# A mixing product's sums of two terms, made by accumulating DMA in place of VectorE

## The chip, the cores and the metric

The kernel runs on one core of a Trainium2 chip. The metric is the device time of one execution in microseconds (us). Engines are called PE (TensorE, matmuls), DVE (VectorE), ACT (ScalarE), POOL (GpSimd) and SP (SyncE, which here only issues DMA). SP and POOL each feed a DMA queue of their own; both queues use the same 16 DMA engines.

## The reference

Three layers, each on the output of the one before, all in float32:

```python
# 1: x (4, 3072, 256): FFT along the sequence, complex mixing, soft threshold, inverse
X = rfft(x, axis=1)
Yr = Xr @ w_r - Xi @ w_i + b_r;  Yi = Xr @ w_i + Xi @ w_r + b_i
Y = sign(Y) * max(abs(Y) - 0.01, 0)          # for each part
x = irfft(Yr + 1j * Yi)
# 2: gated layer with a product along the sequence
h = max(x @ w_in, 0);  u, v = h[..., :512], h[..., 512:]
v_n = (v - mean(v)) / sqrt(var(v) + 1e-6)
v_s = einsum('ts,bsd->btd', w_spatial, v_n) + b_spatial[None, :, None]
x = (u * v_s) @ w_out
# 3: on tokens
g = s * max(x @ w_in2, 0) ** 2 + b
out = g @ w_out2
```

The change lies at the product of `w_spatial` (3072 x 3072) with `v_n` (3072 x 512 for each of four batches), called the mixing product.

## The kernel before

Three stages follow each other: `attention` (the FFT layer, u's input, and v normalized and stored as `vn`), `mixing` (the mixing product), and `output` (everything behind it). The order of instructions on each engine is that of the program; no scheduler moves any.

Mixing computes a 2x2-block product by seven products in place of eight, twice nested. A round is one of the seven outer products; its left factor is a block of `w_spatial` or a sum or difference of several, its right factor the same of `vn` blocks. `OUTER` (line 707) lists, for each round in order (1, 5, 2, 6, 3, 7, 4), the first term of each factor, the second term with its operator, and the name under which the sum is kept for a later round (s1, s2, t1, t2). Inside a round, seven inner products (`INNER`, in the order 2, 5, 3, 1, 6, 7, 4) of six steps each run on the round's quarters. So a round has 42 steps, counted 0 to 41 here, and the stage 294. A step (`multiply`, line 847) is 24 matmuls.

A quarter is six tiles: a11 to a22 are the left factor's (128x768, 384 KB a tile), b11 to b22 the right factor's (128x512, 256 KB). There is one set of them. As soon as a quarter's last use in a round is over (`LAST`), its tiles are loaded again for the next round; `FIRST_USE` gives the inner product in which it is needed there. a12 comes free from step 10 on, a11 from 16, b21 and b12 from 22, a21 and b11 from 28, a22 and b22 from 34, one tile of each a step.

What step n issues, in this order: the 24 matmuls; ACT's rounded high parts of step n + 2 (`high`); DVE's inner sums of step n + 3 (`sums`); at the end of an inner product, `evacuate` for two of four accumulators; DVE's low parts of step n + 2 (`low`); `evacuate` for the other two; the sums of two outer terms (`outer_sums`); a weight conversion, if one is under way; the loads that are due (`loads`).

`evacuate` (line 865) either copies an accumulator into a `kept` tile on ACT (line 877), or adds it to one on DVE (line 873) and stores that to `md` through POOL (line 874). The kept tiles are few: those that ACT writes after a round's first inner product (step 5) are read by the product stores after its fourth (step 23), are written again at step 35, and are read again by the product stores of step 41. So the next round's step 5 can write them once these have landed.

A tile with two terms takes two loads through SP, into the quarter and into a staging tile `st_a` or `st_b` (three of each, lines 765 and 771). Three steps later DVE adds them (line 774), and if the sum is kept, POOL stores it (line 776). `loads` counts the sums under way and leaves further loads of that kind for later steps. Terms by round:
- rounds 1 (outer product 5) and 3 (outer product 6): two terms for all 48 tiles, all sums kept
- round 4 (product 3): two for a only; round 5 (product 7): two for a and b; round 6 (product 4): two for b only; no sum kept
- rounds 0 and 2: one term

The loads of a round run during the round before it.

Of the kernel before, what the change touches and what calls it, by code (L numbers as in the profile page):

```python
# [227 lines left out]
def attention(tc, nc, x, w_r, w_i, b_r, b_i, c_f, c_b, c_g, c_v, c_s, zd, vd, yd, vn, chunks, cd, follow, nb=NB):  # L228
# [338 lines left out]
    def v_product():  # L567

        n = v_done[0]
        v_done[0] += 1  # L570
        y = y_hl[n // 3]
        o = (n % 3) * 128
        pool, tag = (pm, "pm") if tail[0] and n % 2 else (pa, "pa")
        ps = pool.tile([128, 512], F32, tag=tag, name="ps_vp")
        c = 0
        for k in range(2):
            for a, w in PASSES:
                nc.tensor.matmul(ps, y[:, a, k, o:o + 128], win[k][:, w, :], start=c == 0, stop=c == 5)  # L578
                c += 1
        vr = vpool.tile([128, 512], F32, tag="vr", name="vr", bufs=VR)  # L580
        bn = vpool.tile([128, 6], F32, tag="bn", name="bn")
        j = n % 3
        if j == 0:
            grp[0] = (vpool.tile([128, 3, 2], F32, tag="mv", name="mv"),
                      vpool.tile([128, 5, 3], F32, tag="rs", name="rs"), [])
        mv, t, vrs = grp[0]
        vrs.append(vr)
        va, r, z, root, nmr = (t[:, m, :] for m in range(5))

        def stats():  # L590
            nc.vector.bn_stats(bn, vr)  # L591
            nc.vector.bn_aggr(mv[:, j, :], bn)

        def spread():
            nc.vector.tensor_scalar_add(va, mv[:, :, 1], EPS)

        def rstd():
            nc.vector.reciprocal(r, root)
            for _ in range(2):
                nc.vector.tensor_mul(z, r, r)  # L600
                nc.vector.scalar_tensor_tensor(out=z, in0=z, scalar=-0.5, in1=va, op0=ALU.mult, op1=ALU.mult)
                nc.vector.scalar_tensor_tensor(out=r, in0=z, scalar=1.5, in1=r, op0=ALU.add, op1=ALU.mult)
            nc.vector.scalar_tensor_tensor(out=nmr, in0=mv[:, :, 0], scalar=-1.0, in1=r, op0=ALU.mult, op1=ALU.mult)

        def normal(m):
            if m == 0 or m == 2 and n // 3 % 2 == 0:
                nc.scalar.activation(vrs[m], vrs[m], AF.Identity, bias=nmr[:, m:m + 1], scale=r[:, m:m + 1])
            else:
                nc.vector.tensor_scalar(vrs[m], vrs[m], r[:, m:m + 1], nmr[:, m:m + 1], op0=ALU.mult, op1=ALU.add)

        def store():
            b, i = divmod(n - 2, 24)
            for m in range(3):
                nc.gpsimd.dma_start(out=vn[b][i + m], in_=vrs[m])
        ch.step()
        nc.scalar.activation(vr, ps, AF.Relu)
        rest = [wait, stats]
        if j == 2:
            rest += [spread, lambda: nc.scalar.sqrt(root, va), rstd, lambda: (normal(0), normal(1)),
                     lambda: normal(2), store]  # L620
        ch.add(rest)
# [82 lines left out]

OUTER = {
# [7 lines left out]
}  # L715
INNER = (2, 5, 3, 1, 6, 7, 4)

# [12 lines left out]
def mixing(tc, nc, ws, vn, md, sd, convert_half):  # L730
# [31 lines left out]
    def load(g, name, i):  # L762
        first, then = OUTER[outer[g]][0 if name[0] == "a" else 2:][:2]
        t = q[name, i]
        nc.sync.dma_start(out=t, in_=source(first, name, i))
        if then is None:
            return
        op, second, kept = then
        n = t.shape[1]
        s = banks[2].tile([128, n], F32, tag="st_" + name[0], name="st_" + name[0], bufs=3)  # L770
        nc.sync.dma_start(out=s, in_=source(second, name, i))

        def add():
            nc.vector.tensor_tensor(out=t, in0=t, in1=s, op=getattr(ALU, op))
            if kept:
                nc.gpsimd.dma_start(out=sd[kept][int(name[1]) - 1, int(name[2]) - 1, i], in_=t)
        added.append((now[0], name[0], add))

    todo = []

    def loads():

        n = {"a": 3, "b": 3}
        for _, kind, _ in added:
            n[kind] -= 1
        for x in sorted(todo):
            g, _, i, name = x
            if OUTER[outer[g]][1 if name[0] == "a" else 3] is not None:
                if n[name[0]] <= 0:
                    continue  # L790
                n[name[0]] -= 1
            todo.remove(x)
            load(g, name, i)

    def outer_sums(age):
        while added and added[0][0] <= now[0] - age:
            added.pop(0)[2]()

    sub, add = nc.vector.tensor_sub, nc.vector.tensor_add
    term, hl = {}, {}  # L800
# [95 lines left out]
    def run():  # L896
# [12 lines left out]
        for n in range(total):  # L909
            now[0] = n  # L910
            multiply(n)
            ends = n % NS == NS - 1
            if n + 2 < total:
                high("a", n + 2)
                high("b", n + 2)
            if n + 3 < total:
                sums(n + 3)
            if ends:
                evacuate(n, 0)
                evacuate(n, 1)  # L920
            if n + 2 < total:
                low("a", n + 2)
                low("b", n + 2)
                freed(n + 2)
            if ends:
                evacuate(n, 2)
                evacuate(n, 3)
            outer_sums(3)
            if conversion and (todo or n % 3 == 2):
                conversion.pop()()  # L930
            loads()
            if n >= 6 and not conversion and not added and not todo and n % 3 == 0:
                conversion = [x for x in [convert_half(stage)] if x]
# [11 lines left out]
def output(tc, nc, yd, md, chunks, cd, bs, s_in, b_in, out):  # L945
# [43 lines left out]
    def combine(n):  # L989

        c = blocks[n][3]
        into = mixed[n] = m[{"11": 2, "12": 3, "22": 5, "21": 4}[c]]
        sums = {"11": ((2, 1, 2),), "12": ((6, 1, 6), (3, 3, 5), (3, 3, 6)),
                "22": ((7, 6, 7), (5, 5, 7)), "21": ((4, 4, 7),)}[c]
        t = bias_t[n].unsqueeze(1).to_broadcast([128, 2, TH])
        return [z for e in (0, 2) for z in [
            lambda e=e, o=o, x=x, y=y: nc.vector.tensor_add(o[:, e:e + 2], x[:, e:e + 2], y[:, e:e + 2])
            for o, x, y in ((m[o], m[x], m[y]) for o, x, y in sums)] + [
            lambda e=e: nc.vector.tensor_tensor(out=into[:, e:e + 2], in0=into[:, e:e + 2], in1=t, op=ALU.add)]]

    y_t, bias_t = {}, {}
# [223 lines left out]
```

## Time and profile before

| | |
|---|---|
| time, median of 3 runs | 3201.36 us (3199.89 to 3202.3) |
| profiled execution | 3198.43 us, span 3196.7 us |
| mean granted clock of PE | 0.987 of full speed |
| PE busy | 3085.7 us, 97% of the span |
| DVE busy | 2309.5 us, 72% |
| ACT busy | 1428.3 us, 45% |
| POOL busy | 392.8 us, 12% |
| HBM read, written | 322.72 MB, 162.53 MB |
| mixing stage (first to last matmul of line 856) | 559 to 1832 us |

Matmuls are pipelined, so "busy" on PE does not say how many it starts; the number of matmuls in a window does. A window's DMA share is the mean busy share of the 16 DMA engines, and can stand a little over 1. The granted clock is that of PE, as a share of its full speed.

### The profile page before, as it was taken

To read this page: it belongs to the slowest core of one execution; us is meant where nothing else is said; L and a number is where in the kernel's file an instruction comes from. 1 tells how busy PE (TensorE), PEld (TensorE's weight loads), DVE (VectorE), ACT (ScalarE), POOL (GpSimd) and SP (SyncE) were. 2 spreads that over 40 slices of the span, in tenths; PEclk is the share of its full clock that TensorE was granted. 3 is DMA by queue.
4 is the path that set the end of the run, shared out by engine and by line. 5 is a ranking of instruction groups with operands and counts; after the bars stand their busy time and mean duration, and the time that the engine had idled before them with its cause. 6 is when DMAs were issued, how large, how long until landed. Compare 5 with 4: busy or idle time off the path is not lost.

```text
span 3196.7 us, 46508 instructions
## 1 busy us (share of the span) xinstructions
PE 3085.7 (97%) x17960; PEld 3012.8 (94%) x17960; DVE 2309.5 (72%) x3495; ACT 1428.3 (45%) x2244; POOL 392.8 (12%) x497
## 2 busy tenths in 40 slices
PE   6989998999999999999999999999999999999999
PEld 5888986999999999999999989999999999999999
DVE  5877988787878888888878755656566656656564
ACT  5776766433434333434434334444444444444443
POOL 2665544021000210000000100000000000000000
PEclk7999999999999999999999999999999999999999
DMA  8987659487456956466471621111111111110210
GB/s 245 291 263 228 228 184 322 162 314 288 159 198 200 359 212 233 148 217 246 158 238 44 239 82 55 48 50 65 55 65 55 65 55 65 55 64 29 70 45 15
DMA packets 230517, 488.30 MB, mean 153 GB/s; under 512 B 22356, under 2 KB 116376, under 8 KB 230296
## 3 DMA queue, kind: packets, MB, share of 16 engines
q1 hardware_dynamic: 197224, 353.51, 33.4%
q0 software_dynamic: 33072, 131.82, 11.2%
q8 instruction: 140, 2.29, 0.3%
q14 instruction: 81, 0.66, 0.1%
HBM read 322.72 MB, written 162.53 MB: 152 GB/s over the span
## 4 chain that ended last, share of the span: by engine, by line
PE 76%; DVE 13%; DMA 5%; ACT 3%; issue 2%; POOL 0%; SPq 0%; ACTq 0%; DVEq 0%; POOLq 0%
PE acc L856 28%; PE ps_h L1066 17%; PE oacc L1087 17%; PE ps_o L1047 4%; PE ps_u L1029 4%; PE ps_m L413 3%; PE ps_vp L578 2%; DMA st_a<-in_moe_w_spatial_dram 2%; DVE a_hl L837 1%; DVE kept L873 1%; DMA st_b<-vn 1%; DVE b_hl L837 1%; DMA st_b<-t 1%; PE ps_g L366 1%; DVE bn L591 1%
## 5 line engine op out<-in xcount | busy, mean ns | idle before, releaser
L856 PE MATMUL acc<-a_hl,b_hl 128*128 128x384 f32 x7056 | 1239.5, 336 | 32.7 <-DVE kept L873 13.3
L856 PEld LDWEIGHTS acc<-a_hl,b_hl 128*128 128x128 f32 x7056 | 1232.9, 189 | 39.3 <-ACT kept L877 13.0
L1066 PE MATMUL ps_h<-x_hl,w 128*128 128x384 f32 x3072 | 580.8, 337 | 1.5 <-ACT x_hl L1050 0.9
L1087 PE MATMUL oacc<-q_hl,w 128*128 128x384 f32 x3072 | 575.4, 336 | 0.6 <-DVE q_hl L1073 0.6
L1066 PEld LDWEIGHTS ps_h<-x_hl,w 128*128 128x128 f32 x3072 | 543.3, 188 | 2.1 <-ACT x_hl L1050 1.3
L1087 PEld LDWEIGHTS oacc<-q_hl,w 128*128 128x128 f32 x3072 | 537.0, 188 | 0.9 <-DVE q_hl L1073 0.8
L833 ACT CAST a_hl<-a 128x768 fp32r<-128x768 f32 x253 | 211.7, 837 | 524.1 <-PE acc L856 436.7
L1073 DVE TENSOR_TENSOR q_hl<-r,q_hl 128x768 fp32r<-128x768 f32 x256 | 245.4, 959 | 230.7 <-ACT q_hl L1072 230.7
L1071 DVE TENSOR_TENSOR r<-r 128x768 f32<-128x768 f32 x256 | 244.8, 956 | 204.4 <-ACT r L1070 204.4
L1072 ACT CAST q_hl<-r 128x768 fp32r<-128x768 f32 x256 | 213.7, 835 | 301.8 <-DVE r L1071 301.8
L1070 ACT ACTIVATE r<-ps_h 128x768 f32<-128x768 f32 x256 | 208.3, 814 | 310.6 <-PE ps_h L1066 307.2
L837 DVE TENSOR_TENSOR a_hl<-a,a_hl 128x768 fp32r<-128x768 f32 x253 | 241.4, 954 | 137.5 <-ACT a_hl L833 137.0
L837 DVE TENSOR_TENSOR b_hl<-b,b_hl 128x512 fp32r<-128x512 f32 x295 | 202.0, 685 | 0.0
L833 ACT CAST b_hl<-b 128x512 fp32r<-128x512 f32 x295 | 181.8, 616 | 0.0
L578 PE MATMUL ps_vp<-win,y_hl 128*128 128x512 f32 x576 | 154.5, 404 | 18.3 <-ACT v_sb L444 15.0
L874 POOL DMA_DIRECT2D md<-kept x112 | 60.7, 542 | 828.4 <-DVE kept L873 824.0
L1029 PE MATMUL ps_u<-y_hl,w 128*128 128x384 f32 x768 | 145.7, 339 | 1.8 <-DVE y_hl L1015 1.8
L1047 PE MATMUL ps_o<-g,w 128*128 128x384 f32 x768 | 139.2, 337 | 1.6 <-DVE g L1037 1.0
L578 PEld LDWEIGHTS ps_vp<-win,y_hl 128*128 128x128 f32 x576 | 102.1, 190 | 40.4 <-ACT v_sb L444 16.8
L1029 PEld LDWEIGHTS ps_u<-y_hl,w 128*128 128x128 f32 x768 | 135.5, 190 | 3.1 <-DVE y_hl L1015 2.1
L1047 PEld LDWEIGHTS ps_o<-g,w 128*128 128x128 f32 x768 | 133.4, 188 | 2.6 <-DVE g L1037 1.6
L873 DVE TENSOR_TENSOR kept<-acc,kept 128x768 f32<-128x768 f32 x112 | 102.9, 952 | 22.1 <-PE acc L856 21.1
(139 smaller groups left out, 3700.7 us busy)
## 6 DMA issues: line engine op xcount, KB each, us to landing
a<-in_moe_w_spatial_dram SPq DMA_DIRECT2D x144, 384.0 KB, 5.0
b<-vn SPq DMA_DIRECT2D x168, 256.0 KB, 5.3
md<-kept POOLq DMA_DIRECT2D x112, 384.0 KB, 5.3
m<-md SPq DMA_DIRECT2D x56, 768.0 KB, 5.6
st_a<-in_moe_w_spatial_dram SPq DMA_DIRECT2D x72, 384.0 KB, 6.4
vn<-vr POOLq DMA_DIRECT2D x96, 256.0 KB, 4.0
s<-a POOLq DMA_DIRECT2D x48, 384.0 KB, 5.8
x_f<-in_x_dram SPq DMA_DIRECT2D x32, 384.0 KB, 6.5
```

What stands on the lines that cost most here:

```text
L578: nc.tensor.matmul(ps, y[:, a, k, o:o + 128], win[k][:, w, :], start=c == 0, stop=c == 5)
L833: nc.scalar.copy(s[:, 0, :], t)
L837: sub(s[:, 1, :], term.pop((kind, n)), f(s)[:, 0, :])
L856: nc.tensor.matmul(acc[d][:, h, 0:TH], b[:, m, d * 128:(d + 1) * 128], a[:, w, h * TH:(h + 1) * TH], start=fresh and i == 0 and c == 0, st ...
L1029: nc.tensor.matmul(ps[:, d, 0:TH], win[k][:, a, o:o + 128], y[:, w, k, :], start=c == 0, stop=c == 5)
L1047: nc.tensor.matmul(ps[:, h, 0:TH], wo[k // 2][:, a, o:o + 128], g[:, w, k, :], start=c == 0, stop=c == 11)
L1066: nc.tensor.matmul(ps[:, e, 0:TH], w[:, a, o:o + 128], x[:, i, j, :], start=c == 0, stop=c == 5)
L1070: nc.scalar.activation(r, ps[:, :, 0:TH], AF.Relu)
L1071: nc.vector.tensor_mul(r, r, r)
L1072: nc.scalar.copy(s[:, 0], r)
L1073: nc.vector.tensor_sub(s[:, 1], r, f(s)[:, 0])
L1087: nc.tensor.matmul(ps[:, h, 0:TH], w[:, a, o:o + 128], s[:, i, e, :], start=ff == 0 and c == 0, stop=ff == 2 * NP - 1 and c == 2)
```

## The change

A second term is no longer loaded into a staging tile and added by DVE. Its DMA adds to the quarter's tile directly (`accum_op=ALU.add`), issued by POOL four steps behind the first term's load. The store of a kept sum follows three steps behind that, also by POOL. `loads` no longer counts sums under way; it takes up to three loads a step. Since such a DMA only adds, the subtractions are made by signs: half of the `vn` blocks are stored negated (the second Newton step of the normalization multiplies two constants by the sign), and `combine` in the output stage takes the signs back (`tensor_sub` for `tensor_add` in places, as many instructions as before).

```diff
-            for _ in range(2):
+            for s in (1.0, sign):      # sign = -1.0 if (b < 2) == (i >= 12) else 1.0
                 nc.vector.tensor_mul(z, r, r)
-                nc.vector.scalar_tensor_tensor(out=z, in0=z, scalar=-0.5, in1=va, ...)
-                nc.vector.scalar_tensor_tensor(out=r, in0=z, scalar=1.5, in1=r, ...)
+                nc.vector.scalar_tensor_tensor(out=z, in0=z, scalar=-0.5 * s, in1=va, ...)
+                nc.vector.scalar_tensor_tensor(out=r, in0=z, scalar=1.5 * s, in1=r, ...)
...
-        op, second, kept = then
-        n = t.shape[1]
-        s = banks[2].tile([128, n], F32, tag="st_" + name[0], name="st_" + name[0], bufs=3)
-        nc.sync.dma_start(out=s, in_=source(second, name, i))
-
-        def add():
-            nc.vector.tensor_tensor(out=t, in0=t, in1=s, op=getattr(ALU, op))
-            if kept:
-                nc.gpsimd.dma_start(out=sd[kept][int(name[1]) - 1, int(name[2]) - 1, i], in_=t)
-        added.append((now[0], name[0], add))
+        second, kept = then
+
+        added.append((now[0] + 4, lambda: nc.gpsimd.dma_start(out=t, in_=source(second, name, i), accum_op=ALU.add)))
+        if kept:
+            added.append((now[0] + 7, lambda: nc.gpsimd.dma_start(
+                out=sd[kept][int(name[1]) - 1, int(name[2]) - 1, i], in_=t)))
...
-        n = {"a": 3, "b": 3}
-        for _, kind, _ in added:
-            n[kind] -= 1
-        for x in sorted(todo):
-            g, _, i, name = x
-            if OUTER[outer[g]][1 if name[0] == "a" else 3] is not None:
-                if n[name[0]] <= 0:
-                    continue
-                n[name[0]] -= 1
-            todo.remove(x)
+        for g, _, i, name in sorted(todo)[:3]:
+            todo.remove((g, FIRST_USE[name], i, name))
             load(g, name, i)
...
-    def outer_sums(age):
-        while added and added[0][0] <= now[0] - age:
-            added.pop(0)[2]()
+    def outer_sums():
+
+        for x in [x for x in added if x[0] <= now[0]]:
+            added.remove(x)
+            x[1]()
...
-        sums = {"11": ((2, 1, 2),), "12": ((6, 1, 6), (3, 3, 5), (3, 3, 6)),
-                "22": ((7, 6, 7), (5, 5, 7)), "21": ((4, 4, 7),)}[c]
+        sums = {"11": ((minus, 2, 1, 2),), "12": ((minus, 6, 6, 1), (plus, 3, 3, 5), (minus, 3, 3, 6)),
+                "22": ((minus, 7, 6, 7), (minus, 5, 7, 5)), "21": ((minus, 4, 7, 4),)}[c]
```

How this moves instructions is shown at three places of round 0. On SP, the loads of b21 and b12 from step 22 on, before (st_b is the staging tile, vn0 to vn3 the four batches' `vn`):

```order
L765 DMA b21_6353<-vn2_71 128x512
L771 DMA st_b_8421<-vn0_69 128x512
L765 DMA b12_6365<-vn3_72 128x512
L771 DMA st_b_8424<-vn1_70 128x512
L765 DMA b21_6354<-vn2_71 128x512
L771 DMA st_b_8470<-vn0_69 128x512
L765 DMA b21_6355<-vn2_71 128x512
L771 DMA st_b_8545<-vn0_69 128x512
```

and after:

```order
L770 DMA b21_6353<-vn2_71 128x512
L770 DMA b12_6365<-vn3_72 128x512
L770 DMA b21_6354<-vn2_71 128x512
L770 DMA b12_6366<-vn3_72 128x512
L770 DMA b21_6355<-vn2_71 128x512
L770 DMA b12_6367<-vn3_72 128x512
```

The staging loads are gone from SP, and b12's tiles come one a step instead of waiting for free staging.

On DVE, the accumulators' last evacuation of round 0 (step 41; line 873 before, 868 after) with what stands around it, before:

```order
L774 TENSOR_TENSOR a22_6338<-a22_6338,st_a_9043 128x768
L774 TENSOR_TENSOR b12_6369<-b12_6369,st_b_9046 128x512
L774 TENSOR_TENSOR b11_6376<-b11_6376,st_b_9049 128x512
L873 TENSOR_TENSOR kept_8941<-acc_8967,kept_8941 128x768
L873 TENSOR_TENSOR kept_8945<-acc_8974,kept_8945 128x768
L837 TENSOR_TENSOR a_hl_9192<-a12_6348,a_hl_9192 128x768
L837 TENSOR_TENSOR b_hl_9194<-b21_6354,b_hl_9194 128x512
L873 TENSOR_TENSOR kept_8951<-acc_8981,kept_8951 128x768
L873 TENSOR_TENSOR kept_8955<-acc_8988,kept_8955 128x768
L774 TENSOR_TENSOR a22_6339<-a22_6339,st_a_9086 128x768
L774 TENSOR_TENSOR b12_6370<-b12_6370,st_b_9089 128x512
L837 TENSOR_TENSOR a_hl_9241<-a12_6349,a_hl_9241 128x768
```

and after (L832 is `low`, line 837 before):

```order
L832 TENSOR_TENSOR a_hl_9074<-a12_6347,a_hl_9074 128x768
L832 TENSOR_TENSOR b_hl_9076<-b21_6353,b_hl_9076 128x512
L868 TENSOR_TENSOR kept_8880<-acc_8902,kept_8880 128x768
L868 TENSOR_TENSOR kept_8884<-acc_8909,kept_8884 128x768
L832 TENSOR_TENSOR a_hl_9108<-a12_6348,a_hl_9108 128x768
L832 TENSOR_TENSOR b_hl_9110<-b21_6354,b_hl_9110 128x512
L868 TENSOR_TENSOR kept_8890<-acc_8916,kept_8890 128x768
L868 TENSOR_TENSOR kept_8894<-acc_8923,kept_8894 128x768
L832 TENSOR_TENSOR a_hl_9154<-a12_6349,a_hl_9154 128x768
L832 TENSOR_TENSOR b_hl_9156<-b21_6355,b_hl_9156 128x512
```

Three adds that stood ahead of the evacuation, and those behind it, are gone; only the low parts remain.

On POOL, the product stores of the same step (`md1`) with the stores of kept sums (`s1`, `t1`), before:

```order
L776 DMA s1_80<-a22_6338 128x768
L776 DMA t1_82<-b12_6369 128x512
L776 DMA t1_82<-b11_6376 128x512
L874 DMA md1_73<-kept_8941 128x768
L874 DMA md1_73<-kept_8945 128x768
L874 DMA md1_73<-kept_8951 128x768
L874 DMA md1_73<-kept_8955 128x768
L776 DMA s1_80<-a22_6339 128x768
L776 DMA t1_82<-b12_6370 128x512
L776 DMA s1_80<-a22_6340 128x768
L776 DMA t1_82<-b22_6341 128x512
L776 DMA t1_82<-b22_6342 128x512
```

and after, where L775 rows are the accumulating DMAs and L777 the stores of kept sums:

```order
L777 DMA s1_80<-a21_6364 128x768
L777 DMA t1_82<-b11_6376 128x512
L775 DMA a22_6337<-in_moe_w_spatial_dram 128x768
L775 DMA b22_6343<-vn1_70 128x512
L869 DMA md1_73<-kept_8880 128x768
L869 DMA md1_73<-kept_8884 128x768
L869 DMA md1_73<-kept_8890 128x768
L869 DMA md1_73<-kept_8894 128x768
L777 DMA s1_80<-a22_6335 128x768
L777 DMA t1_82<-b22_6341 128x512
L775 DMA a22_6338<-in_moe_w_spatial_dram 128x768
L775 DMA b22_6344<-vn1_70 128x512
```

The accumulations are new in POOL's row; the product stores now stand behind those of a22_6337 and b22_6343 and behind the stores of the last a21 and b11 tiles.

## Rows read from the trace of the kernel before

**Rows 1.** Groups by line: busy us, mean ns of one, idle before.

```profile
L856 PE MATMUL acc<-a_hl,b_hl 128*128 128x384 f32 x7056 | 1239.5, 336 | 32.7 <-DVE kept L873 13.3 <-ACT kept L877 9.9 <-ACT vr L616 5.2
...
L774 DVE TENSOR_TENSOR a<-a,st_a 128x768 f32<-128x768 f32 x96 | 91.4, 953 | 18.6 <-DMA st_a<-in_moe_w_spatial_dram 18.6
...
L774 DVE TENSOR_TENSOR b<-b,st_b 128x512 f32<-128x512 f32 x96 | 64.1, 686 | 22.4 <-DMA st_b<-vn 12.4 <-DMA st_b<-t 9.9
...
L874 POOL DMA_DIRECT2D md<-kept x112 | 60.7, 542 | 828.4 <-DVE kept L873 824.0 <-DVE b_hl L837 2.9 <-DVE c_w L143 1.0
```

**Rows 2.** Windows: us, PE PEld DVE ACT POOL busy, clock, DMA share, GB/s.

```profile
640.00:660.00 20.00, 20.00 (x117) 20.00 (x116) 14.74 (x21) 8.98 (x13) 2.71 (x5) 1.00 0.90 287
700.00:720.00 20.00, 17.60 (x103) 17.28 (x101) 14.32 (x20) 6.22 (x10) 5.42 (x10) 1.00 1.03 412
720.00:740.00 20.00, 19.18 (x109) 18.86 (x110) 13.86 (x18) 9.08 (x13) 5.42 (x10) 1.00 1.03 414
740.00:760.00 20.00, 15.05 (x75) 14.76 (x74) 15.23 (x21) 4.06 (x6) 5.96 (x11) 0.83 1.04 415
```

**Rows 3.** Timeline of DVE at step 41: start, us, instruction, idle before.

```profile
745.74 0.96 DVE L774 TENSOR_TENSOR a<-a,st_a 128x768 f32<-128x768 f32 x1 [0.78 <-DMA st_a<-in_moe_w_spatial_dram]
747.41 0.69 DVE L774 TENSOR_TENSOR b<-b,st_b 128x512 f32<-128x512 f32 x1 [0.71 <-DMA st_b<-vn]
749.60 0.69 DVE L774 TENSOR_TENSOR b<-b,st_b 128x512 f32<-128x512 f32 x1 [1.50 <-DMA st_b<-vn]
750.21 1.81 DVE L873 TENSOR_TENSOR kept<-acc,kept 128x768 f32<-128x768 f32 x2
```

**Rows 4.** Timeline of PE at the end of step 41.

```profile
741.69 4.67 PE L856 MATMUL acc<-a_hl,b_hl 128*128 128x384 f32 x26
751.31 4.89 PE L856 MATMUL acc<-a_hl,b_hl 128*128 128x384 f32 x15 [4.95 <-DVE kept L873]
```

**Rows 5.** Windows of 4 us, same columns.

```profile
752.00:756.00 4.00, 4.00 (x14) 4.00 (x14) 4.00 (x6) 0.00 (x0) 1.56 (x4) 0.53 1.03 412
756.00:760.00 4.00, 4.00 (x25) 4.00 (x24) 3.15 (x6) 1.35 (x2) 1.15 (x3) 1.00 1.04 419
```

**Rows 6.** Waits from 700 to 760 us: total, times, longest.

```profile
DVE a L774 <- DMA st_a<-in_moe_w_spatial_dram: 8.3, 7, 2.0
DVE b L774 <- DMA st_b<-vn: 8.2, 6, 3.1
...
PE acc L856 <- DVE kept L873: 5.0, 1, 5.0
...
PE acc L856 <- ACT kept L877: 3.2, 2, 2.4
```

**Rows 7.** Windows at the ends of rounds 2 and 4, same columns.

```profile
1080.00:1100.00 20.00, 17.75 (x101) 17.11 (x100) 14.97 (x19) 8.70 (x13) 5.96 (x11) 1.00 1.03 415
1100.00:1120.00 20.00, 16.49 (x95) 16.04 (x93) 11.13 (x15) 6.60 (x10) 4.34 (x8) 1.00 1.04 413
1120.00:1140.00 20.00, 17.66 (x87) 17.69 (x88) 14.65 (x20) 4.08 (x6) 5.42 (x10) 0.83 1.03 396
1460.00:1480.00 20.00, 20.00 (x117) 20.00 (x117) 16.54 (x23) 6.34 (x10) 1.07 (x2) 1.00 1.02 383
```

**Rows 8.** DMA issues from 620 to 770 us: count, size, us to landing.

```profile
s<-a POOLq DMA_DIRECT2D x24, 384.0 KB, 5.8
a<-in_moe_w_spatial_dram SPq DMA_DIRECT2D x21, 384.0 KB, 8.8
st_a<-in_moe_w_spatial_dram SPq DMA_DIRECT2D x21, 384.0 KB, 10.1
...
md<-kept POOLq DMA_DIRECT2D x16, 384.0 KB, 6.4
```

**Rows 9.** Waits from 840 to 920 us.

```profile
DVE c_w L143 <- DMA c_w<-in_moe_w_in_dram: 11.0, 3, 5.7
```

More of the change, by code (lines that the diff above doesn't have):

```diff
@@ L595, in spread @@
             nc.vector.tensor_scalar_add(va, mv[:, :, 1], EPS)
+        b, i = divmod(n, 24)
+        sign = -1.0 if (b < 2) == (i >= 12) else 1.0
         def rstd():
             nc.vector.reciprocal(r, root)
-            for _ in range(2):
+            for s in (1.0, sign):
                 nc.vector.tensor_mul(z, r, r)
-                nc.vector.scalar_tensor_tensor(out=z, in0=z, scalar=-0.5, in1=va, op0=ALU.mult, op1=ALU.mult)
-                nc.vector.scalar_tensor_tensor(out=r, in0=z, scalar=1.5, in1=r, op0=ALU.add, op1=ALU.mult)
+                nc.vector.scalar_tensor_tensor(out=z, in0=z, scalar=-0.5 * s, in1=va, op0=ALU.mult, op1=ALU.mult)
+                nc.vector.scalar_tensor_tensor(out=r, in0=z, scalar=1.5 * s, in1=r, op0=ALU.add, op1=ALU.mult)
             nc.vector.scalar_tensor_tensor(out=nmr, in0=mv[:, :, 0], scalar=-1.0, in1=r, op0=ALU.mult, op1=ALU.mult)
@@ L927, in run @@
                 evacuate(n, 3)
-            outer_sums(3)
+            outer_sums()
             if conversion and (todo or n % 3 == 2):
@@ L992, in combine @@
         into = mixed[n] = m[{"11": 2, "12": 3, "22": 5, "21": 4}[c]]
-        sums = {"11": ((2, 1, 2),), "12": ((6, 1, 6), (3, 3, 5), (3, 3, 6)),
-                "22": ((7, 6, 7), (5, 5, 7)), "21": ((4, 4, 7),)}[c]
+        plus, minus = nc.vector.tensor_add, nc.vector.tensor_sub
+        sums = {"11": ((minus, 2, 1, 2),), "12": ((minus, 6, 6, 1), (plus, 3, 3, 5), (minus, 3, 3, 6)),
+                "22": ((minus, 7, 6, 7), (minus, 5, 7, 5)), "21": ((minus, 4, 7, 4),)}[c]
         t = bias_t[n].unsqueeze(1).to_broadcast([128, 2, TH])
         return [z for e in (0, 2) for z in [
-            lambda e=e, o=o, x=x, y=y: nc.vector.tensor_add(o[:, e:e + 2], x[:, e:e + 2], y[:, e:e + 2])
-            for o, x, y in ((m[o], m[x], m[y]) for o, x, y in sums)] + [
+            lambda e=e, op=op, o=o, x=x, y=y: op(o[:, e:e + 2], x[:, e:e + 2], y[:, e:e + 2])
+            for op, o, x, y in ((op, m[o], m[x], m[y]) for op, o, x, y in sums)] + [
             lambda e=e: nc.vector.tensor_tensor(out=into[:, e:e + 2], in0=into[:, e:e + 2], in1=t, op=ALU.add)]]
```

10 rows, old and new, of the table OUTER are left out of this document.

## Prediction

> **What bounds the kernel now.** I read the windows first. TensorE (PE) is busy 97% of the span (table above), so only the places where it falls short can be won or lost. The mixing stage runs from 559.5 to 1831.9 us with 7056 matmuls of one kind [rows 1]. In an undisturbed 20 us, PE starts 117 of them [rows 2], so one costs 0.171 us and a step of 24 costs 4.1 us. What a stretch lost is then its missing matmuls times 0.171 us, with idle time and half-clock time both included.
>
> Two stretches matter, at the ends of rounds 0 and 2, whose loads prepare rounds 1 and 3. Those two rounds need a second term for every tile and also a stored sum. From 700 to 760 us PE starts 103, 109 and 75 matmuls where 351 would fit [rows 2]: 64 missing, 10.9 us. From 1080 to 1140 us it starts 101, 95 and 87 [rows 7]: 68 missing, 11.6 us. In both the DMA share is 1.03 or more at 396 to 415 GB/s: the DMA engines are full. Together they lose 22.5 us.
>
> How the full DMA reaches PE is seen at step 41. VectorE (DVE) runs in program order and stands at adds of line 774 whose staging tile has not landed [rows 3]; the longest group of its waits in that stretch is this one, 8.3 and 8.2 us [rows 6]. Behind those adds stands line 873, which empties an accumulator; PE cannot begin step 42 without it and idles 4.95 us [rows 4, 6]. Then the granted clock falls: 0.53 from 752 to 756 us with 14 matmuls, and 25 in the next 4 us [rows 5]. That is the lower of the clock's two levels (1.2 of 2.4 GHz), and it costs about another 2 us for such an idle.
>
> Round 4 loads two terms for every tile of round 5 but stores no sums; at 1460 to 1480 us DMA stands at 1.02 and PE still starts its 117 [rows 7]. So two transfers per tile just fit and three do not. The third large loss, around 840 to 920 us, has another cause, DVE waiting for raw weights to convert (11.0 us in all) [rows 9]; round 1 loads single terms only, and the change does not touch it.
>
> **The change part by part.** Sums of the output stage change operator and operand order, not number or shape, and the second Newton step has two constants negated: nothing, with no cover needed.
>
> Removed: 192 DVE adds, 91.4 + 64.1 = 155.5 us [rows 1], with their waits. Where PE is full they lie beside it and give nothing; in the two bad stretches they are what blocks line 873. So the gain is capped by the 22.5 us, which all comes back if nothing else is late there. Also removed: 192 loads on SP with their waits for a free staging tile. Behind them stood the later first loads, which now leave SP in their own step.
>
> Added: the same 192 transfers on Pool as accumulations, each waiting for the first load that it adds to, and the 96 stores of sums move to three steps behind. Issuing costs Pool about 0.54 us each [rows 1] and Pool is 12% busy: nothing. But Pool is in order. Behind an accumulation or a store that waits stand the four product stores of line 869 (874 before), and for those waits ScalarE: the kept tile written at the end of inner product 2 is the one that the product stores at the end of the round before read. So there is a new chain: accumulation late, product store late, ScalarE's copy late, PE late. The count of weight conversions in the loop stays 40; some start three steps later, nothing.
>
> What remains is the price of an accumulation on full DMA engines, and no row has one. A lower bound is a plain copy of the same bytes, 1x, since in the full stretches time goes by bytes: about 412 GB/s whatever the mix of loads and stores, so 0.954 us for 384 KB and 0.636 us for 256 KB. I see no reason for less: all source bytes still come in. The upper bound is three passes, 3x: both operands in and the sum out. I take 2x, an estimate: to bring two operands to an adder the kernel before spends two transfers of 384 KB (a and st_a [rows 8]), and here also two operands, source and tile, must come into the DMA engine, while writing goes along with reading as in any copy.
>
> The Trainium skill, "Collectives: The Full Stack", section on the bandwidth ceiling and the fold count, says that a reducing transfer is not slowed by its add but by its two source reads, and has it at 32.35 against 62.28 GB/s for a copy, a ratio of 1.93; no run here shows that yet. By that page the sum below would come out about 4 us lower, at 3214 us.
>
> Now the ledger of the heavy part, from the loads of step 22 of round 0 to the product stores of step 41, in DMA time at 412 GB/s, all that stands ahead in program order:
> - first loads of steps 22 to 39: 12 a and 24 b tiles, 26.7 us
> - product stores at steps 23, 29, 35, 41: 16 of 384 KB ([rows 8] has 16 in this part of the run), 15.3 us
> - stores of sums issued up to step 40: 12 a and 18 b, 22.9 us
> - accumulations issued up to step 40: 13 a and 21 b, 25.8 us at 1x
> That is 64.9 us plus 25.8 us times the price: 90.7, 116.5 or 142.3 us at 1x, 2x and 3x. ScalarE needs the kept tile at the end of step 47, 26 steps after the start of step 22, 106.6 us; less some 3 us for the last landing and the copy, 104 us.
>
> At 1x all is there 13 us early, and both losses vanish. At 2x it is late by 12.5 us. Part of that is met already at step 45, when DVE, in order, waits for the first accumulated a22 with the low parts of step 47 behind it; it is the same delay, in two idles of some 6 us. From there each step needs one accumulated pair and one stored pair, 2 x 1.59 + 1.59 = 4.77 us of DMA against 4.1 us of PE, 0.7 us late per step, some 3 us until the round's last tile. Two idles near 5 us cost about 2 us of half clock each, 4 us. So 12.5 + 3 + 4 = 19.5 us are lost at each heavy round in place of 11.25 us on average: +8.25 us, twice, **+16.5 us**.
>
> At 2x round 4 still fits: without stores of sums it is 26.7 + 15.3 + 51.6 = 93.6 us of 104. The other rounds carry less.
>
> The profiled execution took 3198.4 us (span 3196.7 and 1.7 around it), 2.9 us under the median of 3201.4. On it the sum gives 3214.9 us; carried to the median, 3217.9, so **3218 us**.
>
> **The rivals.**
> 1. An accumulation costs about what a copy does. Then DVE's block is gone, the ledger closes early, and up to 22.5 us come back: 3179 us on the median. For it: the ledger at 1x has 13 us of room, and the last use of each tile lies 11 steps behind its load, while before DVE waited three steps behind it. Against it: the second operand's bytes have to come through engines that are already full. The point from which it decides: 64.9 + 25.8p - 104 + 7 = 11.25 gives p = 1.68; below that the kernel gets faster.
> 2. An accumulation costs three passes, or stalls for other reasons to that size. Late by 38 us in each heavy round, plus (3 x 1.59 + 1.59 - 4.1) = 2.3 us over five steps, 11 us, plus 6 us of clock: 55 us against 11.25, twice, +88 us. Round 4 then needs 119.4 us of 104, some +19 us with its clock. 3308 us. For it: nothing in the trace excludes it. Against it: reading and writing run together in every copy here.
> 3. The change moves the stall without moving the time. With p between 1.6 and 1.75 the wait for staging is replaced by an equal one for the product stores; the removed 155.5 us of DVE were beside PE anyway: 3201 us. That is also what "does not do what it says" would look like.
>
> **How the numbers follow.** Forecast (2x, 3206 to 3235) 0.42; rival 1 0.34; rival 2 and prices well above 2x 0.14; rival 3 0.10. A measurement of this kernel can tell about 0.2%, 6.4 us, from no change. Faster gets rival 1 and a little of rival 3, 0.35; same most of rival 3 and the edge of the forecast, 0.11; slower 0.54. The forecast's own range is 3206 to 3235. For 8 in 10 the range must take in rival 1, down to 3174 (22.5 us and a few of the small losses in rounds 0 and 2), and prices up to about 2.8x, 3285.
>
> **What would show it.** The two stretches decide, 700 to 790 and 1080 to 1160 us. If I am right, DVE no longer waits for a landing three steps behind a load; DMA stays at 1.03 for some 20 us longer; PE's idle there ends on ScalarE's copy to kept or DVE's first sums of the next round, which wait for accumulating DMAs; Pool's product stores at the round's end start several steps late. The accumulations' DMA time for their bytes gives the price: well under 1.7 makes rival 1 right and me wrong, near 3 rival 2. Round 4 should show no loss. Losses at 840 to 920 us and in the output stage should be as before; if these move, something else is at work.

## The result and the profile after

The changed kernel takes **3221.3 us** (median of 4 runs, 3216.2 to 3228.1) against 3201.1 us for the kernel before on the same chip, a ratio of 1.0064 with a 95% interval of 1.0045 to 1.0084: slower by 0.6%, 3 us from the forecast of 3218. The profiled execution took 3222.6 us, span 3220.5.

Stage by stage, the mixing stage ran from 559.5 to 1831.9 us [rows 1 has its matmuls] and now runs from 558.9 to 1852.9 us, 21.6 us longer. The rest of the span gained 2.2 us. So the place is the one predicted. The windows of the heavy rounds in the kernel after (columns: us, then PE, PEld, DVE, ACT and POOL busy with their instructions, granted clock, DMA share, GB/s) answer to [rows 2, 7]:

```profile
740.00:760.00 20.00, 20.00 (x118) 20.00 (x117) 8.91 (x12) 5.42 (x8) 10.97 (x16) 1.00 1.07 319
760.00:780.00 20.00, 9.16 (x42) 8.42 (x41) 6.80 (x9) 2.71 (x4) 11.37 (x17) 0.74 1.08 279
780.00:800.00 20.00, 17.60 (x92) 17.60 (x93) 9.26 (x14) 7.16 (x10) 9.82 (x15) 0.91 1.06 313
800.00:820.00 20.00, 15.06 (x81) 13.50 (x80) 19.66 (x38) 8.95 (x15) 0.63 (x2) 1.00 0.47 158
...
1140.00:1160.00 20.00, 10.65 (x54) 10.23 (x53) 3.74 (x5) 1.82 (x3) 11.81 (x17) 0.79 1.08 281
1160.00:1180.00 20.00, 16.12 (x80) 15.80 (x79) 9.02 (x13) 7.16 (x10) 11.07 (x17) 0.87 1.07 301
1180.00:1200.00 20.00, 15.60 (x81) 13.41 (x79) 17.49 (x35) 6.01 (x11) 1.79 (x4) 1.00 0.43 143
...
1480.00:1500.00 20.00, 20.00 (x117) 20.00 (x117) 9.20 (x12) 6.96 (x11) 8.63 (x10) 1.00 1.07 308
```

Three things are to be seen. First, the old losses at the end of rounds 0 and 2 are gone: 740 to 760 us has all 118 of its matmuls, where it had 75 [rows 2]. Second, a larger loss follows one to three windows later: 42 + 92 + 81 = 215 of 351 matmuls, 136 missing, 23.3 us by 0.171 us each, against 10.9 before; and again 54 + 80 + 81 = 215 of 351, 23.3 us, from 1140 to 1200 us, against 11.6. Third, DMA stands at a share of 1.06 to 1.08 but moves only about 280 to 320 GB/s, where a share of 1.03 to 1.04 moved 412 to 415 before [rows 2]. The engines are as full as before and carry fewer bytes.

The timeline of PE in the kernel after (start, us, instruction, and in brackets the idle time before it and what ended it) shows what the loss is made of:

```profile
754.79 8.66 PE L851 MATMUL acc<-a_hl,b_hl 128*128 128x384 f32 x49
772.37 5.71 PE L851 MATMUL acc<-a_hl,b_hl 128*128 128x384 f32 x22 [8.92 <-DVE a_hl L832]
782.40 18.85 PE L851 MATMUL acc<-a_hl,b_hl 128*128 128x384 f32 x98 [4.32 <-ACT kept L872]
801.59 4.70 PE L851 MATMUL acc<-a_hl,b_hl 128*128 128x384 f32 x24 [0.34 <-DVE a_hl L832]
807.52 4.36 PE L851 MATMUL acc<-a_hl,b_hl 128*128 128x384 f32 x22 [1.23 <-DVE a_hl L832]
815.24 10.00 PE L851 MATMUL acc<-a_hl,b_hl 128*128 128x384 f32 x56 [3.36 <-ACT kept L872]
```

Two idles, 8.92 and 4.32 us, together 13.2. After each the matmuls run slowly for a while: 22 in 5.71 us in place of 3.76, and 98 in 18.85 in place of 16.76, 4.0 us in all; the granted clock of 760 to 780 us is 0.74, a mean over the chip's two levels. The other 6.0 us lie between 800 and 820 us (36 missing matmuls there), where DVE is 98% busy and DMA only at 0.47. This we read as DVE catching up on what it could not do while it stood, weight conversions among it; no run varied it by itself, but a kernel whose DVE did not stand carries a burst of the same kind without loss (the plain-copy kernel below).

Who was late is in the timelines of DVE, of ScalarE and of Pool in the kernel after, in that order:

```profile
739.21 2.00 DVE L868 TENSOR_TENSOR kept<-acc,kept 128x768 f32<-128x768 f32 x2 [2.77 <-PE acc L851]
...
742.60 1.82 DVE L868 TENSOR_TENSOR kept<-acc,kept 128x768 f32<-128x768 f32 x2
...
769.88 0.96 DVE L804 TENSOR_TENSOR a<-a,a 128x768 f32<-128x768 f32 x1 [16.80 <-DMA a<-in_moe_w_spatial_dram]
...
1154.62 0.96 DVE L804 TENSOR_TENSOR a<-a,a 128x768 f32<-128x768 f32 x1 [17.23 <-DMA s<-a]
```

```profile
781.55 3.58 ACT L872 COPY kept<-acc 128x768 f32<-128x768 f32 x4 [4.57 <-DMA md<-kept]
```

```profile
760.65 0.89 POOL L775 DMA_DIRECT2D a<-in_moe_w_spatial_dram  x1 [1.24 <-DMA a<-in_moe_w_spatial_dram]
...
765.37 0.90 POOL L775 DMA_DIRECT2D a<-in_moe_w_spatial_dram  x1 [1.30 <-DMA a<-in_moe_w_spatial_dram]
...
770.09 0.90 POOL L775 DMA_DIRECT2D a<-in_moe_w_spatial_dram  x1 [1.31 <-DMA a<-in_moe_w_spatial_dram]
...
772.58 1.20 POOL L869 DMA_DIRECT2D md<-kept  x2 [0.33 <-DVE a_hl L832]
```

Line 804 is the first sum of a step of the next round; it waits 16.8 us for an accumulation (line 775). Line 872 is ScalarE's copy of an accumulator to a kept tile; it waits 4.6 us for the product stores that read that tile, and these were issued from 772.58 us although their sums (line 868) were made at 739 and 743 us. In front of them on Pool stood accumulations, one pair and one stored pair every 4.72 us. Both idles end as the prediction said, and 4.72 us is its 4.77. At the second heavy round DVE's first sum waits 17.2 us; there the wait is put down to the store of the tile that the sum overwrites, which stands three steps behind the accumulation.

One thing the prediction did not have stands earlier, at step 23. Pool in the kernel after, its first product store of the round, and the window around it:

```profile
665.25 0.58 POOL L869 DMA_DIRECT2D md<-kept  x1 [14.51 <-DVE kept L868]
```

```profile
660.00:680.00 20.00, 20.00 (x117) 20.00 (x116) 18.87 (x27) 5.93 (x10) 7.87 (x13) 1.00 0.75 223
```

Pool came to this store before its sum was made and stood 14.5 us at it, with the next accumulations behind it in its row, and DMA stood below its full share meanwhile (in the second heavy round Pool stands 11.7 us at the same place). What that cost is seen below, where the product stores leave Pool.

### The profile page after: what moved, and what is told of

Read it like the earlier page. It is cut to its first block, busy times and chain, and to the rows that moved or that the text cites. A ratio compares the mean times of both kernels' runs of the same rounds, so it can differ in the third digit from the quotient of the medians.

```text
span 3220.5 us, 46280 instructions
## 1 busy us (share of the span) xinstructions
PE 3091.6 (96%) x17960; PEld 3016.2 (94%) x17960; DVE 2170.1 (67%) x3303; ACT 1427.7 (44%) x2244; POOL 564.4 (18%) x689
## 4 chain that ended last, share of the span: by engine, by line
PE 75%; DVE 10%; DMA 8%; ACT 3%; issue 2%; POOL 1%; SPq 0%; ACTq 0%; POOLq 0%; DVEq 0%
PE acc L851 27%; PE ps_h L1062 16%; PE oacc L1083 16%; PE ps_o L1043 4%; PE ps_u L1025 4%; PE ps_m L413 3%; DMA b<-t 2%; DMA b<-vn 2%; PE ps_vp L578 2%; DVE kept L868 1%; DVE a_hl L832 1%; DMA md<-kept 1%; DVE bn L591 1%; PE ps_g L366 1%; DMA t<-b 1%
## 5 line engine op out<-in xcount | busy, mean ns | idle before, releaser
L851 PE MATMUL acc<-a_hl,b_hl 128*128 128x384 f32 x7056 | 1243.7, 337 | 50.4 <-DVE a_hl L832 21.6
L832 DVE TENSOR_TENSOR a_hl<-a,a_hl 128x768 fp32r<-128x768 f32 x253 | 241.7, 955 | 239.7 <-ACT a_hl L828 239.6
L832 DVE TENSOR_TENSOR b_hl<-b,b_hl 128x512 fp32r<-128x512 f32 x295 | 202.2, 685 | 0.0
L578 PE MATMUL ps_vp<-win,y_hl 128*128 128x512 f32 x576 | 153.2, 402 | 17.9 <-ACT v_sb L444 14.5
```

What stands on the lines that cost most here:

```text
L832: sub(s[:, 1, :], term.pop((kind, n)), f(s)[:, 0, :])
L851: nc.tensor.matmul(acc[d][:, h, 0:TH], b[:, m, d * 128:(d + 1) * 128], a[:, w, h * TH:(h + 1) * TH], start=fresh and i == 0 and c == 0, st ...
```

## The experiments

The terms are those of the prediction: first load, accumulation, product stores, stores of kept sums, heavy rounds. Ratios are to the kernel before on the same chip, with 95% intervals; the edits are against the kernel after unless another is named.

**The add taken out of the transfer.** The first run asks whether the add is what costs.

```diff
-        added.append((now[0] + 4, lambda: nc.gpsimd.dma_start(out=t, in_=source(second, name, i), accum_op=ALU.add)))
+        added.append((now[0] + 4, lambda: nc.gpsimd.dma_start(out=t, in_=source(second, name, i))))
```

> The 192 accumulating DMAs become plain DMAs of the same bytes on the same queue, in the same order, with the same waits (the second term overwrites the first in place of being added, so the sums are left out). Price theory (an accumulation holds the DMA engines about twice as long as a copy, and that is what makes the two heavy rounds late): the losses at the ends of rounds 0 and 2 (23.2 and 23.3 us of missing matmuls in the changed kernel) fall under 5 us each, and the time to 3172 to 3185 us. Rival, order theory (POOL's one row, where every transfer waits for those ahead of it, does it whatever a transfer costs): the losses stay over 15 us each, 3208 to 3222 us.

Measured: 3175.8 us (3171.5 to 3177.0), ratio 0.993 (0.9915 to 0.9945). The same windows of this kernel:

```profile
740.00:760.00 20.00, 20.00 (x118) 20.00 (x117) 11.79 (x15) 6.78 (x10) 11.31 (x22) 1.00 1.03 413
760.00:780.00 20.00, 20.00 (x117) 20.00 (x116) 14.31 (x20) 9.76 (x14) 10.82 (x20) 1.00 1.00 381
780.00:800.00 20.00, 20.00 (x117) 20.00 (x116) 18.56 (x36) 9.21 (x15) 0.00 (x0) 1.00 0.26 79
```

At 413 GB/s in place of about 300, DMA is done early and nothing is lost. Same transfers, same queue, same waits: so the 43 us between the two kernels (by their ratios, 1.0064 and 0.993) lie in the add, and order and waits alone do not make the loss. On the chip of the result 0.993 would be 3179 us, the first rival's figure: that is what the change would have been worth at a copy's price. From 780 to 800 us DVE is 93% busy with 36 instructions and PE still starts all its 117: so busy a DVE costs nothing here, where it has not stood before.

**The price alone.** This kernel leaves the computation out and only issues DMAs: from Pool, plain or accumulating, alone or beside plain loads on SP.

> Only DMA: 24 tiles of 384 KB in turn loaded by SP, loaded by POOL, accumulated by POOL; loaded and accumulated by 256 KB; stored; then POOL loads 24 while SP loads 24 others, and POOL accumulates 24 while SP loads 24. All of the network's work is left out. Price theory, 2x: a phase of plain loads takes about 23 us (24 times 0.954), one of accumulations about 46 us, the 256 KB ones 15 and 31 us; two loads side by side 46 us, loads beside accumulations 69 us. Rival with three passes: 69 us for the accumulations, 92 us beside loads. Rival in which the price is not DMA time but a longer landing alone: accumulations take longer by themselves than loads, but beside SP's loads no more than 46 us in all.

One execution. Windows of 10 us (columns: us, DVE and POOL busy, granted clock, DMA share, GB/s), in order: Pool's plain loads of 384 KB, Pool's accumulations of 384 KB, Pool's plain loads beside SP's loads, accumulations beside SP's loads:

```profile
40.00:50.00 10.00, 0.00 (x0) 5.60 (x11) 1.00 1.02 408
90.00:100.00 10.00, 0.00 (x0) 4.30 (x5) 1.00 1.09 209
230.00:240.00 10.00, 0.00 (x0) 0.74 (x2) 1.00 1.03 403
280.00:290.00 10.00, 0.00 (x0) 3.44 (x4) 1.00 1.07 270
```

Alone, 408 against 209 GB/s is a price of 1.95; by spacing (accumulations from 79.14 to 98.08 us, ten steps; loads from 39.76 to 51.48 us, twelve), 1.894 us for an accumulation against 0.977 us for a load, 1.94. That agrees with the 1.93 of the Trainium skill, "Collectives: The Full Stack", section on the bandwidth ceiling and the fold count, which has it for a reduce-scatter against an all-gather between cores. The reason given there, two source reads, is tested by no run here. Beside loads, where half of the bytes are plain, 2 x 403/270 - 1 = 1.99. The share is full, 1.07 to 1.09, in both accumulating stretches. So the price is two; three is excluded, and so is a price that is only a longer landing, which would have left the 403 GB/s beside loads. Issuing an accumulation took Pool 0.86 us against 0.54 us for a plain load, as the issues in these two stretches show:

```profile
49.52 0.54 POOL L89 DMA_DIRECT2D x<-in_moe_w_spatial_dram  x1 [0.44 <-DMA x<-in_moe_w_spatial_dram]
...
98.08 0.86 POOL L89 DMA_DIRECT2D x<-in_moe_w_spatial_dram  x1 [1.03 <-DMA x<-in_moe_w_spatial_dram]
```

The whole run agrees. Queue rows of the page of before (packets, MB, share of the 16 engines):

```profile
q1 hardware_dynamic: 197224, 353.51, 33.4%
q0 software_dynamic: 33072, 131.82, 11.2%
```

and of after:

```profile
q1 hardware_dynamic: 169576, 290.59, 27.2%
q0 software_dynamic: 60720, 194.75, 22.0%
```

62.9 MB moved from SP's queue to Pool's. The two shares together went from 44.6% of 3196.7 us to 49.2% of 3220.5, 158.8 us more at the same bytes. As plain copies the 62.9 MB take 152.7 us at 412 GB/s, or 157.3 us counted at the share of 1.03 that goes with it. So the accumulations cost 1.01 to 1.04 times themselves on top: about 2.0.

**By bytes or by instruction.** Only the left half of each tile is accumulated; the other half keeps the first load's values.

```diff
-        added.append((now[0] + 4, lambda: nc.gpsimd.dma_start(out=t, in_=source(second, name, i), accum_op=ALU.add)))
+        added.append((now[0] + 4, lambda: nc.gpsimd.dma_start(
+            out=t[:, 0:t.shape[1] // 2], in_=source(second, name, i)[:, 0:t.shape[1] // 2], accum_op=ALU.add)))
```

> The changed kernel with each accumulating DMA cut to the left half of its tile (the other half of the second terms is left out); number of instructions, order and waits as in the changed kernel. Price theory, cost by bytes, twice a copy's: half the bytes at twice the price load the DMA engines like plain copies of the whole, so the time is that of the plain-copy run, 3172 to 3182 us, with no loss over 3 us in the heavy rounds. Rival (an accumulation costs by instruction: its longer issue on POOL, its longer way to landing): most of the loss stays, 3200 us and more.

Measured: 3173.4 us (3168.8 to 3175.0), 0.9916 (0.9901 to 0.9931). Half the bytes at twice the price load the ledger like whole copies, and the time is that of whole copies. In the windows of this kernel the heavy stretch is whole:

```profile
740.00:760.00 20.00, 20.00 (x117) 20.00 (x116) 13.65 (x18) 6.18 (x10) 15.42 (x23) 1.00 1.10 325
760.00:780.00 20.00, 20.00 (x118) 20.00 (x117) 15.30 (x25) 9.27 (x15) 8.59 (x13) 1.00 0.80 251
```

The number of accumulations, their order and what they wait for were unchanged, and each held Pool's issue no shorter (0.85 us and more in both kernels), so these are not what costs.

**Pool's order.** The product stores go to SP's queue, so that they no longer stand behind accumulations.

```diff
-            nc.gpsimd.dma_start(out=md[outer[g]][x, y, d], in_=t.rearrange("p h t -> p (h t)"))
+            nc.sync.dma_start(out=md[outer[g]][x, y, d], in_=t.rearrange("p h t -> p (h t)"))
```

> The changed kernel with the product stores (md) issued by SP in place of POOL, nothing else. Price theory: the product stores no longer stand behind late accumulations, so ScalarE's wait for them (second idle of each heavy round, 4.3 and 3.9 us, with its half clock) goes, but the accumulations come no earlier and the first idle (8.9 and 9.4 us) stays: some 4 to 7 us less per heavy round, 3206 to 3215 us. Rival (POOL's row is all of it): both idles go, under 3190 us. Second rival: SP stands at the product stores waiting for VectorE, the first loads behind them leave later, no gain or a loss, 3219 us and more.

Measured: 3232.3 us (3231.0 to 3235.2), 1.0103 (1.0088 to 1.0118): a miss, slower than the kernel after. The heavy rounds gained what was expected in size, 96 matmuls missing from 760 to 820 us and 97 from 1140 to 1200, 16.5 us each in place of 23.3, but in the other idle. PE in the first heavy round, and the window at step 23:

```profile
764.83 4.37 PE L851 MATMUL acc<-a_hl,b_hl 128*128 128x384 f32 x22 [0.99 <-DVE a_hl L832]
773.07 11.16 PE L851 MATMUL acc<-a_hl,b_hl 128*128 128x384 f32 x50 [3.88 <-ACT kept L872]
```

```profile
660.00:680.00 20.00, 20.00 (x118) 20.00 (x117) 18.82 (x27) 5.96 (x10) 3.79 (x6) 1.00 1.05 325
```

The second idle was to go and the first to stay. In fact the first falls from 8.92 to 0.99 us (9.35 to 1.85 in the second heavy round) and the second stays (4.32 to 3.88, 3.88 to 4.26). Pool no longer stands at the product store of step 23, DMA is full from there (325 GB/s where the kernel after moved 223), and the accumulations that DVE waits for land earlier. The kernel lost more at the end of the stage than it gained. PE there:

```profile
1850.85 1.30 PE L1025 MATMUL ps_u<-y_hl,w 128*128 128x384 f32 x3 [10.80 <-DMA w<-cd]
...
1871.33 0.69 PE L1043 MATMUL ps_o<-g,w 128*128 128x384 f32 x1 [11.78 <-ACT g L1032]
```

and the waits of SP's queue there (total, times, longest):

```profile
SPq L869 <- DVE kept L868: 24.4, 5, 20.7
```

SP stood 20.7 us at a product store whose sum was not there yet, with the next stage's weight loads behind it. In windows of 20 us PE starts 25 and 24 matmuls from 1840 to 1880, where the kernel after starts 99 and 67. So some 7 us of each heavy round's loss hang on Pool's order, and by accumulations that stand behind a product store, more than by product stores behind accumulations. On the other side, the stores' place on Pool keeps SP free for loads.

**Fewer bytes in the full stretch.** If DMA time is what lacks, stores that nobody needs soon can leave it. The stores of kept sums, all but those of a21 and b12, are put off to steps 4 to 15 of the next round, three a step; once in the kernel after, once in the kernel before.

```diff
-            added.append((now[0] + 7, lambda: nc.gpsimd.dma_start(
+            (added if name in ("a21", "b12") else late).append((now[0] + 7, lambda: nc.gpsimd.dma_start(
...
+            for _ in range(3 if 4 <= n % 42 < 16 else 0):
+                if late and late[0][0] <= n:
+                    late.pop(0)[1]()
```

> The changed kernel, with the stores of kept sums of a12, a11, b21, b11, a22 and b22 (none of which is overwritten early) moved from seven steps behind the load to steps 4 to 15 of the next round, three a step; those of a21 and b12 stay. Price theory: the same bytes at the same price, but 12 or more us of stores no longer lie ahead of the product stores of step 41 and of the accumulations that step 45 waits for, so the ledger closes (116.5 us less 7.6 us for b21 and b11 and 5.7 us for a11, 103 of 104): the two losses fall from 23 us to under 8 us each, 3176 to 3192 us. Rival: the stores moved into rounds 1 and 3 collide with their loads and weight conversions and the time goes there, 3205 us and more.

> The kernel before (sums on VectorE) with the same stores moved in the same way. If its two losses (10.9 and 11.6 us) come from full DMA engines, through VectorE's wait for a staging tile, they fall under 3 us each: 3178 to 3186 us, and the accumulating DMA then has nothing left to win over it. Rival (VectorE's adds three steps behind their loads come too early in any case): half of the losses stays, 3188 to 3201 us.

In the kernel after: 3198.5 us (3193.0 to 3202.4), 1.0002 (0.9993 to 1.0012), a miss by 6 us. In the kernel before: 3180.2 us (3178.8 to 3186.2), 0.9951 (0.9934 to 0.9968), as expected. The first half of the reason held: the first idle is gone and the second down to 2.5 us. But a new one came. PE, and what DVE waited for from 755 to 845 us, in the kernel after with late stores:

```profile
766.45 25.24 PE L851 MATMUL acc<-a_hl,b_hl 128*128 128x384 f32 x144 [2.52 <-ACT kept L872]
797.63 19.32 PE L851 MATMUL acc<-a_hl,b_hl 128*128 128x384 f32 x96 [5.95 <-ACT kept L872]
```

```profile
DVE c_w L143 <- DMA c_w<-in_moe_w_out_dram: 10.9, 3, 7.0
```

The stores, bunched three to a step, filled DMA again (1.02 at 414 GB/s from 780 to 800 us) just as raw weights were loaded. DVE came to convert these one step after the load, found them not landed, and stood (3.0 of the 10.9 us at 793.71 us); ScalarE's part of the conversion waited for DVE, and its copies of the accumulators to the kept tiles, which PE needed, stood behind that. ScalarE in this kernel:

```profile
795.23 0.41 ACT L155 CAST c_w<-c_w 128x256 fp32r<-128x256 f32 x1 [7.86 <-DVE c_w L149]
```

That is the step of this expectation that failed: a store without a deadline still takes its place in the queue from what has one.

**Spread, with the conversion later.** So two stores a step over steps 4 to 21, and a conversion always two steps behind its load, where it could be one step behind:

```diff
-            if conversion and (todo or n % 3 == 2):
+            if conversion and n % 3 == 2:
```

In the kernel before the condition keeps the early conversion where second terms are due. Both were run on both kernels: spread stores with the later conversion, and the later conversion alone.

> The changed kernel with the late stores spread at two a step and each conversion two steps behind its load. If what was left in the run with three a step was raw weights landing late behind bunched stores (a 6 us idle at 797 us, VectorE waiting 11 us for them), it goes, and the loss in round 1 with it; the short wait for the product stores (2.5 us a heavy round) stays: 3174 to 3186 us. Rival (accumulations still late, whatever the stores do): 3192 us and more. Price theory also has it no better than the kernel before with the same two changes.

> The kernel before with the late stores of kept sums spread at two a step over steps 4 to 21 of the next round, and, in steps where no load with a second term is due, a weight conversion taken up two steps behind its load in place of one. Price theory: the heavy rounds' losses stay gone as with three a step, and VectorE no longer waits for raw weights in round 1 (11.0 us of waits in the kernel before, some 10 us of missing matmuls): 3166 to 3177 us, under both kernels. Rival (the loss in round 1 is VectorE's own load, not the wait): 3178 to 3186 us as with three a step.

> The changed kernel with a conversion taken up two steps behind its load, and nothing else. If the two edits of the spread run are separate things, this takes only round 1's loss (11 us of missing matmuls from 840 to 960 us) and leaves the heavy rounds' 46 us: 3207 to 3215 us. Rival (the conversions' place is what mattered in the spread run): under 3195 us.

> The kernel before with a conversion taken up two steps behind its load where no load with a second term is due, and nothing else: round 1's loss of 10 us goes, the heavy rounds' 22.5 us stay, 3185 to 3194 us. Rival (VectorE is simply full in round 1): no change, 3196 to 3203 us.

| | kernel before | kernel after |
|---|---|---|
| unchanged | 1 | 1.0064 (1.0045 to 1.0084) |
| later conversion | 3191.1 us, 0.9982 (0.9972 to 0.9992) | 3205.8 us, 1.0022 (1.0011 to 1.0033) |
| late stores, three a step | 3180.2 us, 0.9951 (0.9934 to 0.9968) | 3198.5 us, 1.0002 (0.9993 to 1.0012) |
| spread stores and later conversion | 3173.3 us, 0.9918 (0.9903 to 0.9933) | 3171.1 us, 0.9913 (0.9896 to 0.9929) |

The two runs on the kernel before came out inside their ranges; on the kernel after, the spread stores came out 3 us under theirs and the later conversion 1 us under. Both kernels of the last row beat both of this case, and their intervals overlap: with the full stretch relieved, the add's second pass no longer shows in the time. PE in the kernel after with both edits, over what was the heavy stretch:

```profile
772.91 46.04 PE L851 MATMUL acc<-a_hl,b_hl 128*128 128x384 f32 x264 [2.70 <-ACT kept L872]
```

From 760 to 820 us this kernel misses 23 matmuls, 3.9 us, where the kernel after missed 136; most of it is the one idle of 2.70 us. The later conversion alone clears round 1 and leaves the heavy rounds as they were. The kernel after with it:

```profile
760.00:780.00 20.00, 9.40 (x46) 8.66 (x44) 6.07 (x8) 2.71 (x4) 11.15 (x17) 0.83 1.08 275
...
880.00:900.00 20.00, 19.83 (x115) 19.51 (x114) 19.80 (x37) 8.76 (x14) 2.16 (x4) 1.00 0.71 238
```

115 matmuls from 880 to 900 us, where the kernel after starts 99, but 46 from 760 to 780. So the two edits act at two places, and against the later conversion alone the spread stores are worth, by the ratios, 35 us with accumulations (1.0022 to 0.9913) and 20 us with DVE's adds (0.9982 to 0.9918). The larger gain is where DMA was more overloaded.

## Why the prediction was right, and where its sum was off

- **The price.** Taken as 2, an estimate from passes; measured 1.94 alone, 1.99 beside loads, about 2.0 over the run, and by bytes. This decided the sign: the prediction's turning point was 1.68. The second rival's three passes are excluded.
- **The removed adds.** 155.5 us of DVE gave nothing in the full stretches. DVE's busy time went from 2309.5 to 2170.1 us, and the old block at line 774 is gone, as said; the same bytes plus a second pass took its place.
- **The chain.** Both idles came, in the order given: DVE's first sum, then ScalarE's copy behind the product stores. 13.2 us in two idles against 12.5 us late "in two idles of some 6 us", and 4.0 us of half clock against 4. That 12.5 and 13.2 lie so close is in part luck. The ledger lets the DMA engines be full from step 22 on, but Pool stood 14.5 us at the product store of step 23, and the run with the product stores on SP puts some 7 us of the loss there. It also counts 13 accumulations of a tiles where 12 stand behind the loads of step 22, 1.9 us too many at 2x.
- **The size of a heavy round's loss: 23.3 us in each against 19.5.** The term that was mis-sized is the 3 us that were to be lost from there to the round's last tile. In its place 6 us went between 800 and 820 us, with DVE at 98%. The prediction counted DMA's lateness and not that an engine which stands for 16.8 us has its own work still to do; that this is the cause is read from the trace. The two rounds together cost 24.0 us net against 16.5.
- **A loss that went away.** From 1240 to 1260 us the kernel before started 89 of 117 matmuls, and the kernel after starts 118: 4.8 us back that were not forecast. In the kernel before DVE waited 2.0 us there for raw weights to convert, but the later conversion alone leaves the loss (90 of 117). From 1220 to 1260 us all four kernels with DVE's adds miss 28 to 36 matmuls, and none of the seven with the second term by DMA misses more than two. So it goes with the exchange, against the prediction's sentence that the adds give nothing where PE is full; whether by the adds or by the order of the loads was not tried and stays open.
- **The median, 3 us off, is closer than the sum was.** On the profiled executions the kernel after is 24.2 us longer, where the sum said 16.5. The forecast was carried up by 2.9 us to the median of before, and the profiled execution of the kernel after lies 1.3 us above its own median; that the two make up for 4 of the 8 us is luck.
- **What was to stay.** Round 4 loses nothing, 117 matmuls at a DMA share of 1.07. From 840 to 960 us 65 matmuls are missing, 11.1 us, against 60 before; the later conversion clears it on both kernels, so its cause is the conversions, as read from [rows 9].
- **The first rival** was right on its own terms: at a copy's price the kernel takes 3175.8 us, and it gave 3179. **The third** is not what happened; the price is above its 1.6 to 1.75, and the time moved by more than it allows.
- **Issue on Pool**, put at 0.54 us, is 0.86 us for an accumulation. The half-tile run, with as many issues, loses nothing in the heavy rounds by it.

## What to carry to other kernels

Where DMA is the late resource, an accumulating DMA does not replace a load and an add: on DMA time it cost here about what two loads cost, and in the full stretches it freed only an engine that was not the bound. First look for bytes in the full stretch that have no deadline there, and spread them thinly where DMA has room; here that was worth 20 us to one kernel and 35 us to the other. When an in-order engine or queue is made to wait, count what stands behind it and the backlog that it must then work off.

## What the runs showed of the hardware that was not expected

- DMA's share and its GB/s part company with accumulations: 1.09 at 209 GB/s alone, 1.07 at some 310 GB/s in the kernel, against 1.02 to 1.04 at some 410 for copies. Read by GB/s alone, a full DMA looks half empty.
- An accumulation holds Pool's issue for 0.86 us in place of 0.54, and takes 9.2 us from issue to landing in the median for 384 KB over the whole run, where the plain copy in its place takes 6.6.
